# Cached attention decode on one core: the two places of a head's keys in SBUF 48 tiles apart instead of 80, and the value products in another order

## The chip, the cores and the metric

The kernel runs on one core of a Trainium2 chip. The metric is the device time of one execution in microseconds; the time before is the median of three runs. TensorE is PE in the profile (its weight loads are PEld), VectorE is DVE, ScalarE is ACT, GpSimd is POOL, SyncE is SP. SP computes nothing here: it issues the large transfers.

## The reference

One token goes through a pre-normalised attention block with a cache of 32768 keys and values for each of 32 heads, and then through a small dense layer. Cut to what matters (bf16 inputs):

```
x: 1 x 512;  k_cache, v_cache: 32 heads x 32768 x 128;  wq: 512 x 4096;  wo: 4096 x 512
q      = (layernorm(x) @ wq)                    # 32 heads of 128
scores = (q[h] . k_cache[h]) * 128**-0.5        # 32768 for each head
p      = softmax(scores)
o[h]   = p @ v_cache[h]                         # 128 for each head
h      = x + o @ wo
out    = h + mish(layernorm(h) @ w1 + b1) @ w2  # w1: 512 x 1376, w2: 1376 x 512
```

Each head reads 32768 x 128 x 2 bytes = 8.39 MB of keys and as much of values, 537 MB over all heads; everything else is some 11 MB.

## The kernel before, in words

**Tiles.** A head's 32768 positions lie as 128 partitions x 256 columns. A column is a tile of 128 x 128: for each of 128 positions (one in each partition) its 128 numbers. `SCOLS` is 256, `TPS` is 128 (half a head) and `GT` is 8 tiles to a group, so that a head has 32 groups.

**The loop.** `one(n)` is the body for one head and is a hardware loop on PE, DVE and ACT. For each group, `k_group` transposes eight key tiles on PE against an identity (L471) into one of four PSUM tiles `tps`, DVE copies the group to `ering` (L474), and three groups later (`KEEP = 3`) `scores` multiplies the eight copies with the query (L441). When the 256 score columns stand in `S_ps`, `soft_max`, `soft_a` and `soft_b` find the largest score over all partitions (DVE L496, PE L502, DVE L504, PE L507, DVE L509), `soft_exp` takes the exponential on ACT in two pieces (L513, the events `expa` and `exp`), `pv` multiplies the 256 value tiles with the probabilities and accumulates into one PSUM column (L484), `soft_c` sums the exponentials (L519, L521, L522) and `oev` scales the result (L491).

**Where the keys lie.** `ring` is one SBUF tensor. Its first `SCOLS + DYN` = 336 tiles hold keys. A head with an even number lies at tile 0, one with an odd number at tile `DYN` = 80, so that both homes share the `FIX = SCOLS - DYN` = 176 tiles in the middle. A head's score columns 0 to 175 are those shared tiles; they have fixed addresses. The columns from `FIX` on are the 80 tiles that only this home has, at the lower or the upper end by turns. In the loop their address depends on the round, so it stands in a register of PE, set again for each tile. `pbuf` holds the probabilities by the position in the head, not by the score column: the first piece of the exponential covers the shared tiles, the second piece the others. For an even head the second piece is positions 0 to 79, for an odd head positions 176 to 255. Values have one home of 256 tiles after the keys, and the weights lie behind them.

**What orders the transfers.** All large transfers are issued by SP in the order of a list: keys and values of head 0, keys and values of head 1, and so on (`order`, issued at L330). Before each issue SP waits for what `freed_by` names:

```
        if what[0] == "k" and what[2] == 2 and what[1] > 0:
            return [f"free_d{what[1] - 1}"]
        if what[0] in "kv" and what[1] > 0:
            return [f"free_{what[0]}{what[1] - 1}"]
```

The keys of head h + 1 wait for `free_k{h}`, which PE signals with the last transpose of the shared tiles of head h (column `FIX`); the tiles at the ends are another head's. The values of head h + 1 wait for `free_v{h}`, the last product of `pv`. One transfer is a whole head (128 rows of 64 KB), except for the keys of heads 0, 30 and 31, which come in three parts cut at `CUT` (the third one waits for `free_d`, the end of the transposes at the home's own end), and the values of head 31, which come in halves. PE begins a head when all of its keys have landed (`ready["k0"]`), and its value products when all of its values have (`ready["v"]`).

In the texts below T is the moment at which the last bytes of a head's keys have landed, so that PE may begin that head; period means the time from one T to the next.

## Time and profile before

| | |
|---|---|
| median of 3 runs | 1326.34 us (1324.78 to 1326.97) |
| the profiled execution's own time | 1322.51 us |
| span of the profile (first to last instruction) | 1320.7 us |
| time outside the span | 1.81 us |
| mean granted TensorE clock | 0.799 |
| read from HBM | 548.08 MB, 415 GB/s over the span |

The span is what the views of the profile are about. A row of the chain of waits gives a start, a length and what it was; where the row is a DMA, it runs from the issue of the transfer to the moment at which the engine that waited for it could go on. The issue of a transfer is also a row on SP's queue in the timeline, and the view of DMA issues gives for the issues of a window the time from the issue to the landing of the last bytes. In the views of groups, "x8192" is a count, and the figure after the busy time is the mean of one instruction in ns. PEclk is the granted share of the full TensorE clock.

### The profile page before, as it was taken

To read this page: it belongs to the slowest core of one execution; us is meant where nothing else is said; L and a number is where in the kernel's file an instruction comes from. 1 tells how busy PE (TensorE), PEld (TensorE's weight loads), DVE (VectorE), ACT (ScalarE), POOL (GpSimd) and SP (SyncE) were. 2 spreads that over 40 slices of the span, in tenths; PEclk is the share of its full clock that TensorE was granted. 3 is DMA by queue.
4 is the path that set the end of the run, shared out by engine and by line. 5 is a ranking of instruction groups with operands and counts; after the bars stand their busy time and mean duration, and the time that the engine had idled before them with its cause. 6 is when DMAs were issued, how large, how long until landed. Compare 5 with 4: busy or idle time off the path is not lost.

```text
span 1320.7 us, 56019 instructions
## 1 busy us (share of the span) xinstructions
PE 1125.9 (85%) x25131; PEld 1052.0 (80%) x25131; DVE 734.0 (56%) x1279; ACT 28.3 (2%) x134; POOL 5.3 (0%) x98
## 2 busy tenths in 40 slices
PE   4788888998889888889888889988898988898997
PEld 4678787887778887878787778887787877787886
DVE  3465555665545665446655546654466554566662
ACT  0000000000000000000000000000000000000000
POOL 0000000000000000000000000000000000000000
PEclk9787778887778887778877778877788777888776
DMA  9999999999999999999999999999999999999997
GB/s 410 428 433 417 413 421 437 441 413 401 427 415 413 443 403 423 415 411 443 405 421 417 411 417 409 415 431 411 397 433 425 409 419 411 413 443 394 411 431 282
DMA packets 13213, 548.28 MB, mean 415 GB/s; under 512 B 1328, under 2 KB 2704, under 8 KB 3344
## 3 DMA queue, kind: packets, MB, share of 16 engines
q1 hardware_dynamic: 13128, 548.08, 97.9%
q8 instruction: 10, 0.16, 0.1%
q14 instruction: 3, 0.02, 0.0%
q0 software_dynamic: 64, 0.00, 0.0%
q10 hardware_dynamic: 8, 0.00, 0.0%
HBM read 548.08 MB, written 0.00 MB: 415 GB/s over the span
## 4 chain that ended last, share of the span: by engine, by line
DMA 56%; PE 43%; DVE 1%; issue 1%; ACT 0%; ACTq 0%; SPq 0%; DVEq 0%
DMA ring<-in_A_k_cache_dram 56%; PE tps L471 32%; PE sps L441 8%; PE ops L484 2%; PE yps L558 0%; DVE ering L474 0%; PE hlp L507 0%; PE sps L575 0%; PE tps L591 0%; PE hlp L502 0%; DVE pmax L496 0%; PE hlp L519 0%; ACT pbuf L513 0%; DVE gmax L504 0%; PE hlp L401 0%
## 5 line engine op out<-in xcount | busy, mean ns | idle before, releaser
L471 PE MATMUL tps<-identb,ring 128*128 128x128 bf16 x8192 | 782.4, 234 | 96.3 <-DMA ring<-in_A_k_cache_dram 94.3
L474 DVE COPY ering<-tps 128x1024 bf16<-128x1024 bf16 x1024 | 683.5, 691 | 245.1 <-PE tps L471 243.7
L471 PEld LDWEIGHTS tps<-identb,ring 128*128 128x128 bf16 (+1 forms) x8192 | 595.3, 104 | 151.2 <-DMA ring<-in_A_k_cache_dram 96.8
L441 PE MATMUL sps<-qcur,ering 128*128 128x1 bf16 x8192 | 344.0, 164 | 7.1 <-DVE ering L474 6.6
L441 PEld LDWEIGHTS sps<-qcur,ering 128*128 128x128 bf16 x8192 | 310.5, 97 | 9.9 <-DVE ering L474 9.3
L484 PEld LDWEIGHTS ops<-pbuf,ring 128*128 128x128 bf16 x8192 | 229.7, 105 | 45.7 <-ACT pbuf L513 42.6
L484 PE MATMUL ops<-pbuf,ring 128*128 128x1 bf16 x8192 | 227.5, 165 | 43.9 <-ACT pbuf L513 40.8
L491 DVE TENSOR_TENSOR oT<-ops,rtotc 128x1 f32 x32 | 5.1, 161 | 159.1 <-PE ops L484 159.1
L521 DVE TENSOR_REDUCE etot<-hlp 128x1 f32<-128x2 f32 x32 | 5.1, 159 | 108.5 <-PE hlp L519 108.5
L513 ACT ACTIVATE pbuf<-sps,nbias 128x176 f32 x64 | 22.9, 363 | 1268.1 <-DVE nbias L509 1268.1
L507 PEld LDWEIGHTS hlp<-gmax,onesmat 1*128 1x128 f32 x64 | 12.5, 242 | 21.8 <-DVE gmax L504 21.8
L502 PE MATMUL hlp<-ident,pmax 128*1 128x128 f32 x64 | 12.7, 281 | 16.5 <-DVE pmax L496 16.5
L507 PE MATMUL hlp<-gmax,onesmat 1*128 1x1 f32 x64 | 15.2, 305 | 11.8 <-DVE gmax L504 11.8
L496 DVE TENSOR_REDUCE pmax<-sps 128x1 f32<-128x256 f32 x32 | 13.6, 424 | 14.3 <-PE sps L441 14.3
L502 PEld LDWEIGHTS hlp<-ident,pmax 128*1 128x1 f32 x64 | 2.7, 80 | 19.4 <-DVE pmax L496 19.4
L519 PE MATMUL hlp<-esum,onesmat 128*128 128x2 f32 x64 | 18.1, 353 | 0.0
L504 DVE TENSOR_REDUCE gmax<-hlp 1x1 f32<-1x128 f32 x32 | 8.9, 278 | 13.6 <-PE hlp L502 13.6
L519 PEld LDWEIGHTS hlp<-esum,onesmat 128*128 128x128 f32 x64 | 16.1, 312 | 0.0
L509 DVE TENSOR_SCALAR nbias<-hlp 128x1 f32<-128x1 f32 x32 | 5.0, 158 | 18.2 <-PE hlp L507 18.2
L513 ACT ACTIVATION_READ_ACCUMULATOR pbuf<-sps,nbias 128x1 f32 x64 | 12.5, 196 | 0.0
L417 PE MATMUL hlp<-xnT,ring 128*128 128x1 bf16 x128 | 3.5, 165 | 9.9 <-DMA ring<-in_A_wq_dram 9.9
L417 PEld LDWEIGHTS hlp<-xnT,ring 128*128 128x128 bf16 x128 | 3.5, 104 | 10.0 <-issue 10.0
(62 smaller groups left out, 42.5 us busy)
## 6 DMA issues: line engine op xcount, KB each, us to landing
ring<-in_A_k_cache_dram SPq DMA_DIRECT2D x6, 2816.0 KB, 19.3
ring<-in_A_v_cache_dram SPq DMA_DIRECT2D x2, 4096.0 KB, 21.8
ring<-in_A_k_cache_dram SPq DMA_DIRECT2D x3, 2560.0 KB, 18.7
ring<-in_A_wq_dram SPq DMA_DIRECT2D x1, 4096.0 KB, 12.7
ring<-in_A_wo_dram SPq DMA_DIRECT2D x1, 2048.0 KB, 31.2
ring<-in_A_wo_dram SPq DMA_DIRECT2D x1, 1536.0 KB, 34.5
ring<-in_B_w_dram SPq DMA_DIRECT2D x1, 1376.0 KB, 38.3
ring<-in_B_w_dram SPq DMA_DIRECT2D x1, 1280.0 KB, 41.3
```

Of the source, the lines that this page charges most:

```text
L417: S.step(PE, lambda h=h, kc=kc: t_.matmul(Q_REG[:, h:h + 1], wq_v[:, kc, h * Dh:(h + 1) * Dh], xnT[:, 0, kc:kc + 1], start=(kc == 0), stop ...
L441: S.step(PE, lambda r=r: t_.matmul(S_ps[:, col0 + r:col0 + r + 1], ering[:, bg % NE, r, :], qcur[:, :], start=True, stop=True), name=(name ...
L471: S.step(PE, lambda r=r: t_.matmul(tb[:, r * 128:(r + 1) * 128], tile(col0 + r), identb[:, :], is_transpose=True, start=True, stop=True), ...
L474: S.step(DVE, lambda: v.tensor_copy(ering[:, bg % NE, :, :].rearrange("p r d -> p (r d)"), tb[:, :]), name=f"ev{bg}", waits=[f"trb{bg}", f ...
L484: S.step(PE, lambda r=r, last=last: t_.matmul(o_ps[:, 0:1], v_t[:, r, :], pbuf[:, r:r + 1], start=(r == 0), stop=last), name=([f"free_v{h} ...
L491: S.step(DVE, lambda: v.tensor_tensor(oT[:, bass.ds(S.index(h), 1)], o_ps[:, 0:1], rtotc[:, :], ALU.mult), name=f"oev{h}", waits=[f"pv{h}" ...
L496: S.step(DVE, lambda: v.tensor_reduce(pmax[:, :], S_ps[:, 0:SCOLS], AXX, ALU.max), name=f"pmax{h}", waits=[f"qkh{h}"], kind="pmax")
L502: S.step(PE, lambda: t_.matmul(A_REG, pmax[:, :], ident[:, :], start=True, stop=True), name=f"A{h}", waits=[f"pmax{h}", "ident"], kind="A")
L504: S.step(DVE, lambda: v.tensor_reduce(gmax[:, :], A_REG, AXX, ALU.max), name=f"gmax{h}", waits=[f"A{h}"], kind="gmax")
L507: S.step(PE, lambda: t_.matmul(B_REG, onesm[0:1, :], gmax[:, :], start=True, stop=True), name=f"B{h}", waits=[f"gmax{h}", "consts0"], kind ...
L513: return lambda: a.activation(pbuf[:, bass.ds(at(S.counter), c1 - c0)], S_ps[:, c0:c1], ACTF.Exp, bias=nb[:, :], scale=SC, accum_out=esum[ ...
L519: S.step(PE, lambda: t_.matmul(C_REG, onesm[:, :], esum[:, :], start=True, stop=True), name=f"C{h}", waits=[f"expa{h}", f"exp{h}"], kind="C")
```

## The change

Three edits go together.

- `DYN` goes from 80 to 48. The homes lie 48 tiles apart, 208 tiles are shared and 48 are at an end. So `free_k` comes with the transposes of group 25 rather than of group 21 (counted from 0), ten groups with their address in a register become six, the first piece of the exponential has 208 columns rather than 176 and the second 48 rather than 80, and the parts of heads 0, 30 and 31 are 104, 104 and 48 tiles rather than 88, 88 and 80. `ring` becomes smaller by 32 tiles and a rest of 640 elements.
- `pv` goes through the value tiles in the order `PV`: 48 to 127, then 0 to 47, then 128 to 255. The first 80 lie in the first piece of the exponential in both kinds of head, so the first product waits for `expa` alone and the wait for `exp` stands before tile 0.
- `soft_c` stands after 128 products instead of 64.

```
-    NS = 6
-    DYN = 80
+    DYN = 48
     FIX = SCOLS - DYN
     CUT = [0, FIX // 2, FIX, SCOLS]
-    KB, VB, WA, WB_ = (SCOLS + DYN) * Dh, SCOLS * Dh, SLOT, W1 + 640
-    assert (FJ + 1) * D <= DYN * Dh and KB + VB + WA + WB_ == NS * SLOT
+    KB, VB, WA = (SCOLS + DYN) * Dh, SCOLS * Dh, SLOT
+    assert (FJ + 1) * D <= DYN * Dh and DYN < TPS
-    ring = sb([128, NS * SLOT], BF16, "ring")
+    ring = sb([128, KB + VB + WA + W1], BF16, "ring")
...
+        PV = list(range(DYN, TPS)) + list(range(DYN)) + list(range(TPS, SCOLS))
...
-        def pv(h, r0, r1):
-            for r in range(r0, r1):
-                last = r == SCOLS - 1
-                S.step(PE, lambda r=r, last=last: t_.matmul(o_ps[:, 0:1], v_t[:, r, :], pbuf[:, r:r + 1],
-                                                            start=(r == 0), stop=last),
-                       name=([f"free_v{h}", f"pv{h}"] if last else None), kind=("pv" if last else None),
-                       waits=([f"expa{h}", f"exp{h}", (ready["v"], 16 * (h + 1))] if r == 0 else
-                              [(s_half, 16 * (h + 1))] if r == TPS else ()))
+        def pv(h, n0, n1):
+            for n in range(n0, n1):
+                r = PV[n]
+                last = n == SCOLS - 1
+                waits = ([f"expa{h}", (ready["v"], 16 * (h + 1))] if n == 0 else [f"exp{h}"] if r == 0 else
+                         [(s_half, 16 * (h + 1))] if r == TPS else ())
+                S.step(PE, lambda r=r, n=n, last=last: t_.matmul(o_ps[:, 0:1], v_t[:, r, :], pbuf[:, r:r + 1],
+                                                                 start=(n == 0), stop=last),
+                       name=([f"free_v{h}", f"pv{h}"] if last else None), kind=("pv" if last else None), waits=waits)
...
-            pv(h, 0, 64)
+            pv(h, 0, TPS)
             soft_c(h)
-            pv(h, 64, SCOLS)
+            pv(h, TPS, SCOLS)
```

## The prediction, made before the changed kernel ran

> **What bounds the kernel now.** I read the page first, for the engine that has no time to spare, then SP's queue and the chain of waits, for what each transfer waits for.

> ```profile
> span 1320.7 us, 56019 instructions
> PE 1125.9 (85%) x25131; PEld 1052.0 (80%) x25131; DVE 734.0 (56%) x1279; ACT 28.3 (2%) x134; POOL 5.3 (0%) x98
> ...
> DMA  9999999999999999999999999999999999999997
> ...
> q1 hardware_dynamic: 13128, 548.08, 97.9%
> ```

> The DMA engines are busy from end to end, PE is not. So a change of PE's work counts only through the moments at which it releases transfers. These are in SP's queue (issues of values) and in the chain of waits (a DMA row runs from the issue of a head's keys to T):

> ```profile
> 110.59 0.33 SPq L330 DMA_DIRECT2D ring<-in_A_v_cache_dram  x1
> ...
> 627.96 0.33 SPq L330 DMA_DIRECT2D ring<-in_A_v_cache_dram  x1
> ...
> 668.37 0.33 SPq L330 DMA_DIRECT2D ring<-in_A_v_cache_dram  x1
> ```
> ```profile
> 41.16 31.76 DMA ring<-in_A_k_cache_dram
> ...
> 89.09 22.52 DMA ring<-in_A_k_cache_dram
> ...
> 285.15 26.17 DMA ring<-in_A_k_cache_dram
> ...
> 326.37 24.60 DMA ring<-in_A_k_cache_dram
> ...
> 527.20 23.54 DMA ring<-in_A_k_cache_dram
> ...
> 566.92 24.10 DMA ring<-in_A_k_cache_dram
> ...
> 606.16 25.31 DMA ring<-in_A_k_cache_dram
> ...
> 646.80 24.61 DMA ring<-in_A_k_cache_dram
> ...
> 1169.20 26.36 DMA ring<-in_A_k_cache_dram
> ```

> And the view of DMA issues, asked for the values issued at 110.59 and at 627.96, gives their time to landing:

> ```profile
> ring<-in_A_v_cache_dram SPq DMA_DIRECT2D x1, 21.8
> ```
> ```profile
> ring<-in_A_v_cache_dram SPq DMA_DIRECT2D x1, 24.1
> ```

> Period: T is 72.92 for head 1 (41.16 + 31.76) and 1195.56 for head 29, so 28 periods of 40.09 us. Head 15: its keys land at 606.16 + 25.31 = 631.47. The next keys are issued at 646.80, T + 15.3, and the next values at 668.37, T + 36.9. Its own values, issued at 627.96, land 24.1 later, at 652.06; the next keys land at 671.41, 19.35 us after that. Those keys had been issued 5.3 us before the values were through, so 19.35 us is what a transfer of 8.39 MB takes when it follows without a gap (434 GB/s), and two make 38.7. The values had been issued only 3.5 us before the keys landed, and came 20.6 us after them. So 1.4 us of a period are lost, most of it where values follow keys because the values are issued late. What a late issue costs is seen at 110.59: 1.0 us before the keys were through (89.09 + 22.52 = 111.61), and the landing is 21.8 us after the issue. Of these 19.35 are the transfer; 2.4 us pass from the issue on however idle the engines are.

> **Part 1: PE per head.** Groups with a fixed address and groups with an address in a register, from the chain and the timeline:

> ```profile
> 631.52 3.60 PE tps L471 x32
> ...
> 635.95 0.47 PE tps L471 x8
> ...
> 646.30 0.48 PE tps L471 x8
> ...
> 675.24 0.88 PE tps L471 x8
> ...
> 676.30 0.47 PE tps L471 x8
> ```
> ```profile
> 606.89 1.01 PE L471 MATMUL tps<-identb,ring 128*128 128x128 bf16 x8
> ...
> 614.22 0.98 PE L471 MATMUL tps<-identb,ring 128*128 128x128 bf16 x8
> ```

> From 635.95 to 646.30 lie 16 groups of transposes and products: 0.647 us each. From 606.89 to 614.22 lie 7 groups with a register: 1.047 each. Four groups change kind: -1.60 us for each head. At the start of a head the groups are slow as well (675.24 to 676.30, 1.06 us), until the clock comes up; that is not touched.

> **Part 2: the exponential.**

> ```profile
> 619.62 0.41 ACT L513 ACTIVATE pbuf<-sps,nbias 128x176 f32 x1 [38.79 <-DVE nbias L509]
> 619.93 0.19 ACT L513 ACTIVATION_READ_ACCUMULATOR pbuf<-sps,nbias 128x1 f32 x1
> 620.02 0.32 ACT L513 ACTIVATE pbuf<-sps,nbias 128x80 f32 x1
> 620.23 0.20 ACT L513 ACTIVATION_READ_ACCUMULATOR pbuf<-sps,nbias 128x1 f32 x1
> ...
> 620.53 1.85 PE L484 MATMUL ops<-pbuf,ring 128*128 128x1 bf16 x64 [1.28 <-ACT pbuf L513]
> ```

> The products begin 0.10 us after the second piece's last row ends (620.43). With the wait on the first piece alone they begin 0.10 us after 620.12, plus 0.03 for 32 more columns ((0.41 - 0.32) / 96 x 32): -0.28 us. The wait for `exp` now stands behind 80 products (29 ns each by the last row, 2.3 us), while the second piece ends some 0.3 us after the first, so it holds nobody; if it did, 176 products and `soft_c` would be queued behind it, and the next values behind those. `soft_c` 64 products later leaves 128 products, 3.7 us, for two small DVE instructions before `oev`: nothing. So the values' issue moves from T + 36.9 to T + 35.0.

> **Part 3: the keys' issue.** `free_k` comes four fixed groups later: 4 x 0.647 = +2.59 us. SP has nothing else to issue meanwhile: the values behind it in the queue are released 17 us later. T to issue is now 15.05 (311.32 to 326.37) at the least and 16.18 (550.74 to 566.92) at the most; what differs is the number of slow groups. It becomes 17.64 to 18.77.

> This is the step that decides. Values now have time: issued at T + 35.0, with a period over 40, they are 5 us ahead of the next T, as the keys of 646.80 were, and should land at T + 19.35. The keys of the next head are issued at T + 17.6 to T + 18.8, only 0.6 to 1.7 us before that. That is the case of 110.59 with keys and values exchanged. A loop closes through a single head: T, 208 tiles, issue, landing. It takes 17.64 to 18.77 plus 21.8, 39.4 to 40.6; before it was at most 16.18 + 21.8 = 38.0, with room.

> [...]

> For the issue-to-landing time of keys I take 21.8 to 22.1: the row, and a little for one of the 16 engines now and then late. Its floor is 19.35 + a cost below that of values (nothing in the trace shows keys issued so late), its upper end the 24.1 of the values at 627.96, which ran behind engines still at work.

> How often are the slow and the quick ends of 15.05 to 16.18 met? The clock tells:

> ```profile
> 556.00:557.00 1.00, 1.00 (x21) 1.00 (x20) 0.62 (x2) 0.00 (x0) 0.00 (x0) 0.68 0.15 66
> 594.00:595.00 1.00, 1.00 (x24) 1.00 (x22) 1.00 (x2) 0.00 (x0) 0.00 (x0) 0.91 0.15 66
> 635.00:636.00 1.00, 1.00 (x30) 1.00 (x28) 0.85 (x2) 0.00 (x0) 0.00 (x0) 0.93 1.51 655
> 676.00:677.00 1.00, 1.00 (x30) 1.00 (x28) 0.85 (x2) 0.00 (x0) 0.00 (x0) 0.95 0.00 0
> ```

> The third column from the end is the granted clock, which goes from 0.50 to 1.00 once in each of these four stretches: 0.68 is 64% of it at full, so at 556.64, and the others at 594.18, 635.14 and 676.10. The steps between them are 37.5, 41.0 and 41.0, though head 15's period is 39.94 (631.47 to 671.41). They look like points of a grid of 3.4 us (41.0 - 37.5), and 40.96 is 12 of its steps. The later the flip behind T, the longer the slow part: 0.4 us of delay for each us (1 - 0.647 / 1.06), so 15.05 to 16.18 is about one step of the grid. In a loop that closes through the keys, each head's place on the grid follows from the one before: the place moves by 40.96 less the period, which is much for a quick head and little for a slow one, so that slow heads are the more frequent. Iterating this with 17.64 to 18.77 and with 21.8 to 22.1 gives mean periods of 40.2 to 40.8. I take 40.5, +0.4 us on 40.09. 28 heads: +11.4 us.

> **Part 4: the ends.** The first head's keys come in parts of 104 tiles, 16 tiles (1.2 us) later, and its `free_k` moves by that and four groups, 4 to 5.5 us. The next keys were issued at 41.16 and landed at 72.92, 31.76 later, 12.4 over 19.35: the values were before them. Nothing changes there. From T of head 29 on PE sets the end:

> ```profile
> 1195.55:1232.35 36.80, 34.38 (x776) 31.98 (x777) 22.38 (x38) 0.81 (x4) 0.00 (x0) 0.82 0.96 405
> ...
> 1269.14:1306.10 36.96, 34.59 (x775) 32.36 (x773) 22.77 (x39) 0.81 (x4) 0.00 (x0) 0.82 1.00 424
> 1306.10:1320.70 14.60, 8.24 (x232) 6.89 (x231) 3.09 (x16) 0.71 (x3) 0.00 (x0) 0.50 0.35 111
> ```

> Three heads of 36.8 us follow each other without a wait for keys, and 1.88 us less in each makes -5.6. DMA is at 0.96 to 1.00 in the same stretches, so the last weights may now be late: between -3 and -5.6, I take -5.

> **Sum.** Profiled execution: 1322.51 (span 1320.70 and 1.81 around it) + 11.4 - 5.0 = 1328.9. The median lies 3.83 above that execution: 1332.7.

> **The rivals.**
> - Slower still, locked: the period is held at 40.96 us, the distance from flip to flip. It decides once the slowest heads need 40.96, that is 22.2 us from issue to landing behind 18.77. Price 28 x 0.87 = +24.4, less 5: 1345.7. For it: the flips at 594.18, 635.14 and 676.10 and the 24.1 us of the values at 627.96. Against it: 21.8. [...]
> - Faster: the late keys cost less than late values, and the gain at the values stays. If a lead of 0.6 to 1.7 us costs keys only 0.5 us, the period is 19.35 + 19.35 + 0.5 = 39.2: 28 x -0.89 = -25, less 5, 1296. Halfway to the forecast, at 39.85, it is -6.7 - 5: 1314.6, which I take for this case. The point is 40.27, below which the tail's 5 us outweigh the loop. Against it: both kinds are the same 128 rows of 64 KB from the same queue.
> - The loops balance: 40.27 within 0.1, the time stays as it is, about 1326.
> - The change does not reach the release: PE's time falls, but DVE or PE is so slow in the four new fixed groups that the issue is later than 2.6 us. At 1.06 for each, +4.24 instead of +2.59, the period is 42.15: 28 x 2.06 = +57.7, less 5, 1379. The clock is up by then in all heads (676.30), so this is remote.

> **Chances.** Forecast 0.52 (some 0.12 of it inside 0.2%), locked 0.20, faster 0.20, balance 0.04, the last 0.04. 0.2%, 2.7 us, is about what a measurement of this kernel can tell from no change. Faster 0.20; same 0.16; slower 0.64. The range runs from inside the faster case, 1318, of which it leaves out half, to the locked case, 1346, beyond which lies little but the last.

> **What would show it.** Right: T to the keys' issue is 17.6 to 18.8; the values' issue stands 5 us before T and their landing 19.4 after it; keys take 21.8 to 22.2 from issue to landing; PE waits for keys longer than now; the product's wait names ACT for 0.3 us less. Wrong: keys' landings come 19.5 us behind the values' although issued late (then it is faster), or values are still late.

## The result, and the profile after

The changed kernel takes 1337.81 us (median of 5 runs, 1333.97 to 1340.91) against 1326.97 us for the kernel before (5 runs): a ratio of 1.0072, 95% interval 1.0043 to 1.0102. It is slower, by 10.8 us or 0.7%: little, but clear of the scatter. The profiled execution took 1335.53 us, with a span of 1333.7 us and a mean granted clock of 0.767 (before 0.799). The page after, with the parts that answer to those shown of before:

```profile
span 1333.7 us, 54995 instructions
PE 1084.2 (81%) x25131; PEld 1030.1 (77%) x25131; DVE 728.8 (55%) x1279; ACT 28.4 (2%) x134; POOL 5.3 (0%) x98
...
q1 hardware_dynamic: 13128, 548.08, 96.7%
```

PE has 41.7 us less to do and the span is 13.0 us longer. The chain of waits after shows where the time is (a DMA row is from the issue of a head's keys to T):

```profile
45.00 27.94 DMA ring<-in_A_k_cache_dram
...
373.88 21.99 DMA ring<-in_A_k_cache_dram
...
414.72 22.15 DMA ring<-in_A_k_cache_dram
...
455.70 22.08 DMA ring<-in_A_k_cache_dram
...
496.63 22.12 DMA ring<-in_A_k_cache_dram
...
1190.45 22.03 DMA ring<-in_A_k_cache_dram
```

T of head 1 is 72.94 (45.00 + 27.94), of head 29 it is 1212.48: 28 periods of 40.70 us, 0.60 more than before, +16.9 us in all. Head 9 has T = 395.87, and the next keys are issued at 414.72, T + 18.9; they land 22.15 us later. The whole of the period, 41.0, is this loop. The values in SP's queue, and the time to landing of the first of the two issues:

```profile
391.25 0.33 SPq L329 DMA_DIRECT2D ring<-in_A_v_cache_dram  x1
...
432.00 0.33 SPq L329 DMA_DIRECT2D ring<-in_A_v_cache_dram  x1
```
```profile
ring<-in_A_v_cache_dram SPq DMA_DIRECT2D x1, 23.9
```

The values issued at 391.25, 4.6 us ahead of T, land at 415.15, 19.3 us after T: they follow without a gap, and here the loss at the values is gone. The next ones, at 432.00, are 4.9 us ahead of T at 436.87. The keys were issued only 0.4 us before the values' landing, and land 21.7 us after it.

Over 28 heads, before: keys are issued 4.8 us on the mean ahead of the end of the values and land 19.64 us after it, values 2.9 us ahead of the end of the keys and land 20.45 us after it. After the change it is 1.1 us and 21.28 us for the keys, 5.1 us and 19.42 us for the values. The sums are the two periods, 40.09 and 40.70. The loss has moved from the values to the keys and has grown. The waits of PE before and after:

```profile
PE tps L471 <- DMA ring<-in_A_k_cache_dram: 94.3, 30, 5.6
PE ops L484 <- ACT pbuf L513: 40.8, 32, 1.3
```
```profile
PE tps L471 <- DMA ring<-in_A_k_cache_dram: 157.4, 30, 7.9
...
PE ops L487 <- ACT pbuf L514: 30.4, 32, 1.0
```

The figures of a row are the us in total, the number of waits and the longest. PE waits 63.1 us more for keys, in 30 heads, and 10.4 us less for the exponential in 32 heads, 0.33 us in each.

### The profile page after: what moved, and what is told of

It is laid out like the page before. It is cut to its first block, busy times and chain, and to the rows that moved or that the text cites. A ratio compares the mean times of both kernels' runs of the same rounds, so it can differ in the third digit from the quotient of the medians.

```text
span 1333.7 us, 54995 instructions
## 1 busy us (share of the span) xinstructions
PE 1084.2 (81%) x25131; PEld 1030.1 (77%) x25131; DVE 728.8 (55%) x1279; ACT 28.4 (2%) x134; POOL 5.3 (0%) x98
## 3 DMA queue, kind: packets, MB, share of 16 engines
q1 hardware_dynamic: 13128, 548.08, 96.7%
HBM read 548.08 MB, written 0.00 MB: 411 GB/s over the span
## 4 chain that ended last, share of the span: by engine, by line
DMA 54%; PE 45%; issue 0%; DVE 0%; SPq 0%; ACT 0%; ACTq 0%
DMA ring<-in_A_k_cache_dram 51%; PE tps L471 34%; PE sps L441 9%; DMA ring<-in_B_w_dram 3%; PE ops L487 1%; SPq L329 0%; DVE ering L474 0%; PE tps L592 0%; PE hlp L503 0%; PE hlp L508 0%; DVE pmax L497 0%; PE hlp L520 0%; ACT pbuf L514 0%; DVE gmax L505 0%; DVE nbias L510 0%
## 5 line engine op out<-in xcount | busy, mean ns | idle before, releaser
L471 PE MATMUL tps<-identb,ring 128*128 128x128 bf16 x8192 | 736.1, 234 | 159.2 <-DMA ring<-in_A_k_cache_dram 157.4
L471 PEld LDWEIGHTS tps<-identb,ring 128*128 128x128 bf16 x8192 | 566.8, 104 | 191.0 <-DMA ring<-in_A_k_cache_dram 159.9
L487 PEld LDWEIGHTS ops<-pbuf,ring 128*128 128x128 bf16 x8192 | 229.5, 105 | 37.5 <-ACT pbuf L514 33.0
L492 DVE TENSOR_TENSOR oT<-ops,rtotc 128x1 f32 x32 | 5.2, 161 | 105.0 <-PE ops L487 105.0
L514 ACT ACTIVATE pbuf<-sps,nbias 128x208 f32 x64 | 23.0, 363 | 1279.8 <-DVE nbias L510 1279.8
L503 PEld LDWEIGHTS hlp<-ident,pmax 128*1 128x1 f32 x64 | 2.7, 81 | 19.4 <-DVE pmax L497 19.4
L510 DVE TENSOR_SCALAR nbias<-hlp 128x1 f32<-128x1 f32 x32 | 5.1, 158 | 19.6 <-PE hlp L508 19.6
## 6 DMA issues: line engine op xcount, KB each, us to landing
ring<-in_A_k_cache_dram SPq DMA_DIRECT2D x6, 3328.0 KB, 19.6
```

The source lines that it names most:

```text
L471: S.step(PE, lambda r=r: t_.matmul(tb[:, r * 128:(r + 1) * 128], tile(col0 + r), identb[:, :], is_transpose=True, start=True, stop=True), ...
L487: S.step(PE, lambda r=r, n=n, last=last: t_.matmul(o_ps[:, 0:1], v_t[:, r, :], pbuf[:, r:r + 1], start=(n == 0), stop=last), name=([f"free ...
L492: S.step(DVE, lambda: v.tensor_tensor(oT[:, bass.ds(S.index(h), 1)], o_ps[:, 0:1], rtotc[:, :], ALU.mult), name=f"oev{h}", waits=[f"pv{h}" ...
L503: S.step(PE, lambda: t_.matmul(A_REG, pmax[:, :], ident[:, :], start=True, stop=True), name=f"A{h}", waits=[f"pmax{h}", "ident"], kind="A")
L514: return lambda: a.activation(pbuf[:, bass.ds(at(S.counter), c1 - c0)], S_ps[:, c0:c1], ACTF.Exp, bias=nb[:, :], scale=SC, accum_out=esum[ ...
```

## The experiments

In each, "before" is the kernel before, run beside it. The theory: the next keys' issue, 2.6 us later, closes a loop through a single head, T to free_k to issue to landing, which now sets the period. The rivals: the new order of the products costs the time; or a delay of the issue costs nothing and the cause is elsewhere; or the delay acts, but without the clock's grid.

**The order alone** (the changed kernel with the old homes):

```
-    DYN = 48
+    DYN = 80
```

> The changed kernel with its new order of the products, and with the homes 80 tiles apart as before. Theory (the late keys' issue costs the time, through the loop T, free_k, issue, landing): the keys' issue stays at T + 15.6 on average, the values' issue comes 0.3 us earlier (T + 36.9 on average), and the values have a little more lead: 0.1 to 0.3 us less in a period, 1318 to 1324 us. Rival (the new order, with its wait inside the products and its later sum, costs the time): 1337 us or more, as the changed kernel, with PE waiting in front of tile 0 or of the sum.

Measured: 1320.72 us, ratio 0.9967 (0.9946 to 0.9988). The new order is a gain of 0.3%; it isn't what costs.

**The homes alone** (48 tiles, with the old order of the products and the old first wait):

```
-            pv(h, 0, TPS)
+            pv(h, 0, 64)
             soft_c(h)
-            pv(h, TPS, SCOLS)
+            pv(h, 64, SCOLS)
...
+                       waits=([f"expa{h}", f"exp{h}", (ready["v"], 16 * (h + 1))] if r == 0 else
```

> The changed kernel with its homes 48 tiles apart and the old order of the products (first wait on both pieces of the exponential). Theory: the loop through the keys does not contain the products, so the period stays at 40.7 us with the keys' issue at T + 18.3; the values still have 4 to 5 us; only the tail loses 3 x 0.3 us: 1337 to 1340 us. Rival (the new order costs): back to 1327 us or below.

Measured: 1336.54 us, ratio 1.0087 (1.0061 to 1.0113): the changed kernel's time within both intervals. Where keys gate the loop the order is worth nothing that can be seen, since the products aren't in the loop.

**Only the keys later** (the kernel before, with PE's work as it was):

```
-[f"free_k{h}"] if col0 + GT == FIX else
+[f"free_k{h}"] if col0 + GT == FIX + 16 else
```

> The kernel before, with one thing changed: free_k is signalled two groups later (column 192 instead of 176), so that the next keys are issued 2.1 us later while PE's work is what it was. Theory: keys are now late as well as values (T + 17.7 on average), 1.4 us ahead of the values' end: the loss at the keys is added, while a longer period gives the values lead: period 40.6 to 40.9, 1340 to 1350 us. Rival (an issue as early as 1.4 us ahead is enough for keys; the changed kernel is slower for another reason): 1327 us as before.

Measured: 1344.56 us, ratio 1.0145 (1.0110 to 1.0179). A later issue of the keys costs time by itself. In its trace the keys are issued at T + 17.4 on the mean over 28 heads (before 15.6), and the mean period is 40.87, inside the expected 40.6 to 40.9. Single periods go from 39.1 to 42.8. Two long ones:

```profile
376.51 21.89 DMA ring<-in_A_k_cache_dram
...
415.07 24.91 DMA ring<-in_A_k_cache_dram
...
457.79 24.35 DMA ring<-in_A_k_cache_dram
```

The issue is 16.7 us behind T (398.40 to 415.07) and 17.8 behind the next (439.98 to 457.79), and the periods are 41.6 and 42.2. Only the second loses its time at the keys: they are issued 2.0 us ahead of the values' end (459.79) and land 22.4 us after it. In the first it is the values that come late, at 420.40, 22.0 us after T, and the keys follow in 19.6. Both losses are there, in different heads, since the values' issue is still what it was before.

**One group later still** (the changed kernel), which asks whether the clock's grid holds the period:

```
-[f"free_k{h}"] if col0 + GT == FIX else
+[f"free_k{h}"] if col0 + GT == FIX + 8 else
```

> The changed kernel with free_k one group later (column 216 instead of 208, a group with a register address, 1.05 us). Theory with the clock's grid: T to the keys' issue becomes 18.6 to 19.9 by the place on the grid, with 22.0 us to the landing 40.6 to 41.9, and 40.96 lies inside: the flip of the clock stands at one place behind T (3.5 to 4.2 us) in most heads, periods are 40.96 within 0.15, and the time is 1343 to 1350 us. Rival without a grid (a delay of the issue is a delay of the loop): period 40.70 + 1.05 = 41.75, 1365 to 1369 us.

Measured: 1343.98 us, ratio 1.0161 (1.0131 to 1.0191) where the changed kernel has 1.0072: 6.2 us more, as expected with the grid, and far from the rival's 29 us. Its granted clock (third column from the end) in four stretches, and its chain:

```profile
404.00:405.00 1.00, 1.00 (x29) 1.00 (x26) 0.88 (x2) 0.00 (x0) 0.00 (x0) 0.84 0.00 0
445.00:446.00 1.00, 1.00 (x28) 1.00 (x25) 0.92 (x2) 0.00 (x0) 0.00 (x0) 0.86 0.00 0
486.00:487.00 1.00, 1.00 (x26) 1.00 (x23) 0.91 (x2) 0.00 (x0) 0.00 (x0) 0.89 0.00 0
527.00:528.00 1.00, 1.00 (x30) 1.00 (x26) 0.94 (x2) 0.00 (x0) 0.00 (x0) 0.91 0.00 0
```
```profile
377.53 21.77 DMA ring<-in_A_k_cache_dram
418.45 21.82 DMA ring<-in_A_k_cache_dram
459.41 21.78 DMA ring<-in_A_k_cache_dram
500.33 21.96 DMA ring<-in_A_k_cache_dram
```

The flips, where the clock goes from 0.50 to 1.00, are at 404.32, 445.28, 486.22 and 527.18, 40.95 apart on the mean, and the periods are 40.97, 40.92 and 41.10: flip and T go together, with the flip 4.9 to 5.0 us behind T (I had said 3.5 to 4.2). Over the 28 heads of this execution the period is 40.6 to 41.3 (mean 40.92), and the flip stays 3.8 to 5.1 us behind T, where it goes from 2.8 to 6.1 in the changed kernel. The period keeps to the grid: in the loop of the kernels before and after, the flips to 1.00 are 37.55, 40.96 or 44.37 us apart (before: 556.63, 594.18 and 635.14; 754.61 and 798.98), which are 11, 12 and 13 steps of 3.413 us, and the mean period of this run lies 0.04 below 12 steps.

That the time grew by so little isn't shown to be the grid's doing alone. The group was worth less than 1.05 us: heads whose flip is 4.9 us behind T issue the keys at T + 18.38 in the changed kernel and at T + 19.11 here, and the means over 28 heads are 18.32 and 19.05, 0.73 apart. And issue to landing fell, from 22.38 to 21.87 on the mean: in the changed kernel the six landings of 23 us or more belong to keys issued 1.4 to 2.1 us ahead of the values' end, and here all are issued 0.1 to 0.7 us ahead. The difference, 0.22 us in each of 28 heads, is the 6.2 us.

**Halfway** (the changed kernel with 64):

```
-    DYN = 48
+    DYN = 64
```

> The changed kernel with the homes 64 tiles apart, halfway. Theory: keys are issued at T + 17.0 (two fixed groups later than before), values at T + 36.4 or a little less, so that both are issued some 2 to 3 us ahead of the end of the transfer before them; the loop through the keys needs 17.0 + 22.0 = 39.0 and no longer binds alone; both transfers lose a few tenths: period 39.3 to 39.9, which with the tail's 2.5 us gives 1302 to 1319 us. Rival (each later tile of free_k costs its time, in proportion): halfway between the two kernels, 1332 us.

Measured: 1319.34 us, ratio 0.9947 (0.9925 to 0.9968), a little above the top of what I expected and far from the rival's 1332. The mean period, 40.09, is above the 39.3 to 39.9 expected and the same as before in the profiled executions; what that execution gains, 3.6 us, is in the tail after head 29's T (121.6 us against 125.1). The distance of the homes isn't paid by the tile: 80 and the new order 1320.7, 64 1319.3, 48 1337.8. And transfers did not follow each other without loss. Its chain, and the time to landing of the values issued at 469.24 and at 509.46:

```profile
450.28 22.32 DMA ring<-in_A_k_cache_dram
...
489.94 24.42 DMA ring<-in_A_k_cache_dram
...
531.39 21.89 DMA ring<-in_A_k_cache_dram
```
```profile
469.24 0.33 SPq L329 DMA_DIRECT2D ring<-in_A_v_cache_dram  x1
...
509.46 0.33 SPq L329 DMA_DIRECT2D ring<-in_A_v_cache_dram  x1
```
```profile
ring<-in_A_v_cache_dram SPq DMA_DIRECT2D x1, 22.9
```
```profile
ring<-in_A_v_cache_dram SPq DMA_DIRECT2D x1, 24.5
```

The keys issued at 489.94, 2.2 us before the values' end (492.14), land 22.2 us after it; those issued at 531.39, 2.6 us before it (533.96), land 19.3 after it. Two or three microseconds of lead are no safe cover: some transfers lose nothing, others 3 us. Which, these rows do not tell, and it stays open.

**The slow groups behind T taken away.** Identity products at the head of the body keep PE at work where it would wait; they write PSUM columns that nothing reads then.

```
             h = n - 1
+            for _ in range(32):
+                S.step(PE, lambda: t_.matmul(yps[:, 128:256], identb[:, :], identb[:, :], start=True, stop=True))
             for gi in range(2 * GPS):
```

> The changed kernel with 32 products of the identity with itself, written to PSUM columns that nothing reads then, at the head of the loop's body, where PE would wait for keys. They change no result. Theory: PE is busy before T, the clock flips up some 3 us earlier, the slow groups behind T go, the keys' issue moves from T + 18.3 to T + 16.8 to 17.4 without any change of homes; the loop through the keys falls to 38.8 to 39.5 and no longer binds alone: 1300 to 1320 us. Rival (such products do not bring the clock up, or the clock does not matter for the loop): 1338 us, or more by what the products delay the first transposes.

Measured: 1295.50 us, ratio 0.9825 (0.9759 to 0.9891), below the range (three of four runs; the fourth took 1310.79): homes, order and transfers are those of the changed kernel, and 42 us are gone. Of the 18.3 us from T to the issue, some 1.3 on the mean, and 2.1 where the clock is up at T, were half clock. Its chain, then the granted clock (third column from the end) and the first transposes around two of its T (in brackets, PE's wait before them):

```profile
364.94 21.89 DMA ring<-in_A_k_cache_dram
403.09 22.45 DMA ring<-in_A_k_cache_dram
443.45 21.95 DMA ring<-in_A_k_cache_dram
481.66 22.45 DMA ring<-in_A_k_cache_dram
```
```profile
385.00:387.00 2.00, 0.23 (x5) 0.13 (x4) 0.00 (x0) 0.00 (x0) 0.00 (x0) 1.00 1.21 524
424.50:426.50 2.00, 0.91 (x9) 0.91 (x10) 0.00 (x0) 0.00 (x0) 0.00 (x0) 0.50 1.21 524
```
```profile
386.87 1.96 PE L471 MATMUL tps<-identb,ring 128*128 128x128 bf16 x32 [1.77 <-DMA ring<-in_A_k_cache_dram]
...
425.59 3.60 PE L471 MATMUL tps<-identb,ring 128*128 128x128 bf16 x32 [2.11 <-DMA ring<-in_A_k_cache_dram]
```

Issues stand 16.3 and 17.9 us behind T by turns (386.83 to 403.09, 425.54 to 443.45), and periods are 38.71 and 39.86: with the clock up at T (386.83) the keys keep their lead, 3.1 us, and with the clock down (425.54) it is 1.4.

**The same with 64 and 80** (28 and 20 products, new order):

> Homes 64 apart, new order, and 28 such products. Theory: keys issued at T + 15.7, values at T + 35, both 3 us or more ahead of the transfer before them, so that transfers follow without a gap: period 38.7 to 39.2, 1286 to 1302 us. Rival (clock not brought up): as with homes 64 apart alone, 1319 us.

> Homes 80 apart as before, new order, and 20 such products. Theory: keys issued at T + 14.5, values at T + 35.6, 3 us ahead of T: period 38.8 to 39.4, 1289 to 1307 us, a little behind the kernel with 64, since the values' issue is the later one. Rival (clock not brought up): 1321 us.

Measured: 1305.94 us, ratio 0.9870 (0.9843 to 0.9898) with 64, a miss, between the expectation and the rival (the five runs go from 1294.65 to 1310.69); 1321.92 us, ratio 0.9981 (0.9953 to 1.0009) with 80, a miss at the rival's time. In the trace the 20 products take 2.29 us, and the clock comes up 0.7 to 6.0 us behind T, before it in no head.

**More products** (42 with 48, 40 with 64, 32 with 80):

> Homes 48 apart, new order, 42 identity products instead of 32 in front of each head. With 32, heads took 38.71 and 39.7 us by turns: the quick ones had the clock up at T and issued keys 3.1 us ahead of the values' end, the slow ones 1.45 us ahead, with the clock up only 3 to 4 us behind T. Theory: ten more products (105 ns each with the clock down) close the pause before T, the clock is up at T in nearly every head, the keys' issue is at T + 16.3, periods are 38.7 to 38.9: 1278 to 1288 us. Rival (the alternation comes from the transfers themselves, an early transfer being followed by a late one): 1295 us as with 32.

> Homes 64 apart, new order, 40 products instead of 28. Theory: as with 48 and 42; the keys' issue at T + 15 to 15.5, where a later start of PE by up to 0.5 us costs nothing: periods 38.7 to 38.9, and a tail that is 1 to 3 us longer than with 48: 1280 to 1291 us. Rival: 1306 us as with 28.

> Homes 80 apart, new order, 32 products instead of 20. With 20 the clock was up before T + 1 us in few heads, and the time was that of the order alone. Theory (20 products, some 2.1 us, are too short to bring the clock up; 32 with the first transposes are not): the clock is up early in most heads, values' issue at T + 35.5: 1290 to 1308 us. Rival (with homes 80 apart the clock is not what limits, the values are): 1320 us as with 20.

Measured: 1303.31 us, ratio 0.9832 (0.9801 to 0.9863) with 48, a miss: as with 32, heads alternate, and the time can't be told from that with 32. The first transposes of two heads:

```profile
388.74 3.46 PE L471 MATMUL tps<-identb,ring 128*128 128x128 bf16 x32 [2.17 <-DMA ring<-in_A_k_cache_dram]
...
428.31 1.96 PE L471 MATMUL tps<-identb,ring 128*128 128x128 bf16 x32 [0.72 <-DMA ring<-in_A_k_cache_dram]
```

Where PE waits 2.17 us between the products and T, the trace has the clock up 3.2 us ahead of T and down again 0.2 us behind it. Where it waits 0.72 us, the clock stays up. So it came up ahead of T in both heads (the 42 products take 3.80 and 3.74 us, 90 and 89 ns each, where the first 32 transposes take 112 each at half clock and 61 with it up), and was down again just behind T only where the pause was 2.17 us. The other two: 1285.88 us, ratio 0.9681 (0.9656 to 0.9707) with 64, as expected. 1305.68 us, ratio 0.9839 (0.9809 to 0.9870) with 80, as expected, so the products had been too few there. From the chain with 64 and 40:

```profile
567.39 23.79 DMA ring<-in_A_k_cache_dram
591.23 2.06 PE tps L471 x32
...
606.26 23.63 DMA ring<-in_A_k_cache_dram
629.93 1.96 PE tps L471 x32
...
644.86 23.74 DMA ring<-in_A_k_cache_dram
668.64 1.96 PE tps L471 x32
...
1148.01 23.73 DMA ring<-in_A_k_cache_dram
```

The first 32 transposes take 1.96 us, or 2.06 where the clock comes up 0.3 us behind T, and took 3.60 before. T is 629.89, 668.60 and, at the end, 1171.74: 13 periods of 38.70, twice 19.35. The transfers follow each other without a gap; in these heads keys and values are issued 4.1 to 4.8 us ahead. The first 12 heads of this execution, 1297.90 us and the slowest of six, had not yet settled.

**48 products with 64:**

> Homes 64 apart, new order, 48 products instead of 40. With 40, the profiled execution needed 12 heads before its periods settled at 38.70, because the products ended up to 1 us before the keys landed when a head was late. Theory: with 48 they reach T in late heads too, and the period settles within a few heads: 1281 to 1286 us, with less spread between executions. Rival (products that reach beyond T delay the transposes, and keys and values lose their lead): 1290 us or more.

Measured: 1286.89 us, ratio 0.9706 (0.9679 to 0.9733), one microsecond above the expectation and no better than 40; its periods settle after ten heads, not after a few. Both beat the kernel before by 3% and the changed one by 4%.

## Why the prediction was right, point by point

The direction, the mechanism and the range held: 1332.7 forecast, 1337.81 measured. The change was forecast at +6.4 us and came as +10.8; the term that was too small is the keys' time from issue to landing. By its steps:

- **Which transfer is late.** As said: values 4.6 us ahead of T and 19.3 behind it, keys late. That this costs by itself is shown by the keys delayed alone (1.0145), and that nothing else in the change costs by the order alone (0.9967).
- **T to the issue**, forecast 17.64 to 18.77: 18.9 at head 9, and 17.5 to 18.9 over 28 heads (mean 18.3), as one finds by taking T from each issue in the chain. The 40.5 us of the forecast, less 21.8 to 22.1, stand for 18.4 to 18.7, so slow heads are a little less frequent than it took them to be. The delay for each us that the flip comes later, forecast 0.4, is 0.39 over the same heads.
- **Issue to landing**, forecast 21.8 to 22.1: 22.0 to 22.2 in the rows above from 373.88 on; the mean over 28 heads is 22.4, since six took 23.0 to 24.8. This is the term that was too small. Why those six were late stays open.
- **Period**, forecast 40.5 (40.2 to 40.8): 40.70. The size of the change in the loop is 16.9 us where 11.4 were forecast. The six late keys alone lie 8.9 us above 22.1; the somewhat smaller T to issue took part of that back. Two errors of opposite sign make the period look better forecast than its terms were. The rival "locked" was the neighbour: heads 9 to 11 have periods of 41.0, 40.9 and 41.0, and with one group more the mean period was 40.92. In the reading of the clock there is a slip: a stretch at 0.68 has 36% of its time at full clock, not 64%; the flip at 556.64 is placed rightly.
- **PE per head.** The exponential's 0.28 us are 0.33 in the waits. The values' issue moved by 1.6 us (T + 37.2 to T + 35.6 on the mean over 28 heads) rather than 1.9, which cost nothing, since they had 5 us to spare.

ACT's rows after, and the first product:

```profile
423.98 0.43 ACT L514 ACTIVATE pbuf<-sps,nbias 128x208 f32 x1 [39.93 <-DVE nbias L510]
424.31 0.19 ACT L514 ACTIVATION_READ_ACCUMULATOR pbuf<-sps,nbias 128x1 f32 x1
...
424.56 2.59 PE L487 MATMUL ops<-pbuf,ring 128*128 128x1 bf16 x91 [0.95 <-ACT pbuf L514]
```

The first product stands at 424.56, 0.06 us behind the end of the first piece (424.50; forecast 0.10), and nobody waits for the second.

- **The start.** The second keys' issue moved from 41.16 to 45.00, 3.8 us (forecast 4 to 5.5), and T of head 1 stayed (72.92, 72.94), as said.
- **The tail**, forecast -5 (-3 to -5.6): 1333.7 - 1212.5 = 121.2 after, 125.1 before, -3.9. From head 29's T to the end of the last value products it is 105.0 us where it was 110.5: -5.5, close to the -5.6 of PE's three heads. What was lost again has the reason named, the last weights; in the chain and the timeline after:

```profile
1285.84 43.98 DMA ring<-in_B_w_dram
...
1329.96 1.37 PE tps L592 x33
```
```profile
1329.96 1.34 PE L592 MATMUL tps<-ring,actT 128*1 128x128 bf16 x44 [3.17 <-DMA ring<-in_B_w_dram]
```

PE waits 3.17 us for the second layer's weights, which land at 1329.82. Before, it waited 1.59 us at this place, for DVE: so the weights take 1.6 us back.

- **Sum.** Between the two profiled executions: +16.9 - 3.9 = +13.0 (1322.51 to 1335.53). The medians differ by 10.8, since the profiled execution of before lies 4.5 us below its median (1326.97) and the one after 2.3 below its own.
- **The rival "faster"** did not come: late keys cost as much as the row of late values said. With 64 tiles (0.9947) keys and values share the lateness, and the period is no shorter than before. A shorter one came only with the clock up at T.

## What to carry to other kernels

When the transfers are the bound, look at each one for how long before the end of the one ahead of it it is issued: PE's 42 us of saved work bought 3.9 us at the end and nothing in the loop, where an issue 2.7 us later (T + 15.6 to T + 18.3) cost 16.9 us. Freeing work behind a release and moving the release are two effects of one edit, so write down both times. And if the path from landing to release runs on PE behind a stretch in which PE idled, look at the clock granted there (before: 0.50 from 628.00 to 631.50, with no PE instruction, and 3.60 us for the first 32 transposes behind it, where they took 1.96 with the clock up in the kernel with 64 and 40): the identity products were worth 42 us with 48 tiles (32 products), 33 with 64 (40) and 15 with 80 (32), where the placements without them differ by 18.5 at the most.

## What the runs showed of the hardware that was not expected

```profile
306.00:308.00 2.00, 2.00 (x82) 0.50 0.91 393
```

PE is shown as busy throughout, with the clock at half. 40 identity products with 128 columns brought it up between 2.3 us ahead of T and 0.3 behind it in the settled heads (the first 32 transposes took 1.96 us, or 2.06, instead of 3.60), in a kernel that ends 3% sooner.
